# Left-over tokens loaded token by token, b_sg and g_ln loaded at another place, and a new order of the prologue

## The chip, the cores and the metric

The kernel runs on one core of a Trainium2 chip. Its engines work side by side, each through its own queue of instructions: TensorE (PE, with its weight loads PEld), VectorE (DVE), ScalarE (ACT), GpSimd (POOL) and SyncE (SP), which here issues nearly all DMAs. The metric is the device time of one execution in microseconds; the time of the kernel before is the median of three runs, 584.28 us (583.62 to 584.38).

## The reference

Eight heads of attention over pooled keys and values, followed by a gated MLP whose gate mixes the tokens. Cut to what is computed:

```python
# q, k, v: (8, 8, 576, 64)
k_p = k.reshape(B, H, 72, 8, D).mean(axis=3)      # 576 tokens pooled by 8: 72
v_p = v.reshape(B, H, 72, 8, D).mean(axis=3)
attn = softmax(q @ k_p.T / sqrt(D))               # over 72 pooled tokens
x = (attn @ v_p) -> (8, 576, 512)                 # heads side by side
h = gelu_tanh(x @ w_in)                           # w_in: (512, 1024)
u, v = h[..., :512], h[..., 512:]
v_n = (v - mean) / sqrt(var + 1e-6) * g_ln        # over the 512 of v
v_s = einsum('ts,bsd->btd', w_sg, v_n) + b_sg     # w_sg: (576, 576)
out = x + (u * v_s) @ w_out                       # w_out: (512, 512)
```

`w_in` and `w_out` arrive as 64-bit floats (their halves and quarters are loads of 1 MB), everything else as 32-bit.

## The kernel before, in words

**Tiling.** A batch is the unit of work. Four groups g of two heads each go through attention; 576 tokens are five tiles of at most 128. The 72 pooled tokens of a head don't fit two to a tile of 128, so each head's 72 are split into 64 main tokens and 8 left-overs. Main tokens of two heads fill 128 partitions. The left-overs of all eight heads of a batch are collected in one tile, `left`: k's on partitions 96 to 127 (two columns of 32 rows, one for each head of a pair), v's on partitions 64 to 95 (two columns, one for each half of the heads). `load_left` (L256) fills it with four DMAs of 64 KB, each of 32 rows of 2 KB. A row holds the eight tokens of one pooled one. The source is ordered head by head and, within a head, pooled token by pooled token; the partitions of the tile come in the same order.

**Products in three terms.** Matrices are split into a high part that PE multiplies fast and a low remainder, and a product is made of high times high, high times low and low times high. So there are many casts (ACT), subtractions (DVE, POOL) and conversions of the 64-bit weights (L196 to L207, on ACT, DVE, POOL, ACT, POOL in turn).

**Steps.** All work is cut into generator functions, one for each kind of step, and every `yield` ends a piece: A loads two K tiles, B two V tiles, C one group's q, E the left-overs. K pools K (on PE for batch 0, else on DVE, L315), and its third form K2 pools the left-overs of k and v (DVE, L315), transposes them and scales them into `kbd` (ACT, L345, L346). P does the same for V (POOL multiplies the left-overs with a mask, L381; `vl` L393 and L395 follows). Q transposes q. S makes the scores, the softmax (maximum L429, exponentials L441 or L446, sum, reciprocal L458, product L459) and copies the left-overs' probabilities into `el` (POOL, L465). L transposes `el` (PE, L135) and casts it into `lt` (ACT L476, L479, L480; DVE L482). T transposes the other probabilities (L493, L499). V multiplies with V into `x32` (L524) and `xhl`. H makes the v half of h with its normalization (DVE L569 to L575), U the u half, W the mixing over tokens with its eviction (L616, which reads `g_ln` as `gcol` and `b_sg` as `bbc`), O the output product, Z the transposition and the store. Lower-case entries treat the weights: lv, lu, lo load halves of w_in (v, u) and of w_out, `ls0` loads w_sg (five DMAs) and, in the kernel before, behind them `b_sg`, spread over all partitions (288 KB), and `g_ln` (2 KB, element by element); v, u, o, s are their conversions.

**The order.** It is written out by hand in two lists. `PROLOGUE` runs once: it holds batch 0, most of batch 1, the loads and the first pieces of batches 2 and 3, and all weights. `PERIOD` is then run for each further batch. Each entry `K2+1` advances step K2 of batch (period + 1) by one piece, and the instructions of a piece are appended to their engines' queues. At the end the program ties every instruction to the one before it on its engine, so that each engine works strictly in the order of the lists. That holds for SP too: a load that waits for a free buffer holds all loads behind it.

The order of loads on SP in the prologue is, before, A1+0, A0+0, lv0, E0+0, C0+0 to C3+0, lv1, B1+0, B0+0, ls0 (with b_sg and g_ln), E0+1, A0+1, lu0, A1+1, C0+1, C1+1, B0+1, lo0, lu1, B1+1, C3+1, C2+1, C1+2, C0+2, lo1, A1+2, E0+2, A0+2 and so on.

**The mask.** `mask` on partitions 64 to 95 has four columns; column a is 1/8 on the rows of head a of the half, and 0 elsewhere. It is made on POOL by a memset and two selects before the large memsets of `kbd`, `vbh` and others.

Of the kernel before, what the change touches and what calls it, by code (L numbers as in the profile page):

```python
# [35 lines left out]
O1+0 Q2+2 V2+1 V3+1 S0+2 B1+2 A0+3 O0+0 P1+2 Q1+2 S0+2 V3+1 S1+2 O0+0 A1+3 O1+0 P2+2 o3 S1+2 S1+2 S2+2 O2+0 O1+0 S2+2
C3+2 V0+1 S2+2 Z0+0 O2+0 S1+2 o3 V3+1 Z0+0 H2+1 H2+1 Q3+2 C0+3 O2+0 Z1+0 S0+2 T0+2
# [13 lines left out]
def tile_pooled_attn_gmlp(ctx: ExitStack, tc: tile.TileContext, q, k, v, w_in, g_ln, w_sg, b_sg, w_out, out):  # L51
# [46 lines left out]
    def mm(o, lhsT, rhs, start, stop):  # L98
# [112 lines left out]
    def load_wsg():  # L211
        st["ws"] = []
        for i in range(NT):
# [6 lines left out]
            st["ws"].append(w[:n])  # L220
        load(bbc, b_sg.rearrange("(o t) -> o t", o=1).broadcast_to([P, S]))
# [95 lines left out]
    def step_K(b, i):  # L317
# [23 lines left out]
        left = ps[:, 1, 96:P].rearrange("p (g j) -> p g j", g=G)  # L341
# [74 lines left out]
    def step_S(b, g):  # L416
# [47 lines left out]
        for h in range(2):  # L464
            nc.gpsimd.tensor_copy(st["el", b][:, :, JL * (2 * g + h):JL * (2 * g + h + 1)],  # L465
                                  ef[:, :, LEFT[h]:LEFT[h] + JL])
# [277 lines left out]
```

## Time and profile before

| | |
|---|---|
| median of three runs | 584.28 us (583.62 to 584.38) |
| the profiled execution's own time | 584.24 us |
| its span, first to last instruction | 582.5 us |
| granted TensorE clock, mean | 0.991 |
| PE busy | 554.7 us (95%), 3793 matmuls |
| DVE, ACT, POOL busy | 405.6, 351.9, 222.7 us |
| DMA moved | 46.34 MB, mean 80 GB/s |
| chain that ended last | PE 79%, DVE 10%, ACT 4%, DMA 3%, SP 2% |

Times in the profile count from the start of the span. "Busy" of an engine is the union of its instructions' times; an instruction row has start, duration, engine, source line, operation, the tile written and the tiles read, and in brackets the idle time before it with what ended it. Most matmuls come from one helper (L99), so they are told apart by their tiles: `mps` and `aps` are the two rings of PSUM tiles. All loads have line L155, so they go by tile: `kvraw` and `early` are K, V and q of the start, `left` the left-overs, `raw` the 64-bit weights, `stage` w_sg, `bbc` and `gcol` b_sg and g_ln. The busy share is an average over stages with different limits; a stage table shows each.

### The profile page before, as it was taken

Reading aid. Unit: us, or ns where it says so; the run is one execution under the profiler, and the core shown is the slowest. Engines: PE = TensorE matmul, PEld = TensorE weight load, DVE = VectorE, ACT = ScalarE, POOL = GpSimd, SP = SyncE. Lnnn points to the kernel's source line nnn. Section 1 sums busy time; section 2 is a strip of 40 time slices with the busy share of each in tenths; the row PEclk is TensorE's granted clock in tenths of the full one; section 3 lists DMA queues with packets and bytes.
Section 4 is the critical chain, followed back from the end, with each engine's and each line's share of the span. In section 5 each row is a group of like instructions: output and inputs, shape, how many; then the busy total and the mean of one; then the engine's idle time right before and its main releaser. Section 6 shows DMA issues by size and latency. Waiting matters only on the chain.

```text
span 582.5 us, 10319 instructions
## 1 busy us (share of the span) xinstructions
PE 554.7 (95%) x3793; PEld 522.9 (90%) x3793; DVE 405.6 (70%) x555; ACT 351.9 (60%) x1000; POOL 222.7 (38%) x301
## 2 busy tenths in 40 slices
PE   3698988999999999999999999999999999999995
PEld 3576788998999989999999989999999989998995
DVE  0579998988668795778667785688667765344434
ACT  2888776788547775497456765497456775412310
POOL 4365565833326131522416231532417131433230
PEclk9899998999999999999999999999999999999998
DMA  8988460462431634233441724134350211021105
GB/s 199 240 223 236 72 169 27 100 132 47 90 73 37 117 58 97 58 68 51 94 79 37 119 56 96 33 73 72 82 90 1 43 20 21 1 42 22 20 1 82
DMA packets 161282, 46.34 MB, mean 80 GB/s; under 512 B 148752, under 2 KB 148752, under 8 KB 161232
## 3 DMA queue, kind: packets, MB, share of 16 engines
q1 hardware_dynamic: 156464, 45.10, 37.9%
q10 hardware_dynamic: 4768, 0.59, 0.7%
q8 instruction: 30, 0.49, 0.4%
q14 instruction: 20, 0.16, 0.1%
HBM read 36.23 MB, written 9.44 MB: 78 GB/s over the span
## 4 chain that ended last, share of the span: by engine, by line
PE 79%; DVE 10%; ACT 4%; DMA 3%; SPq 2%; issue 1%; ACTq 0%; POOL 0%; DVEq 0%
PE mps L99 65%; PE aps L99 11%; PE aps L135 3%; ACT e L446 2%; SPq L155 2%; DMA left<-in_v 1%; DMA qraw<-in_q 1%; DVE e L459 1%; DVE bst L569 1%; DVE nmax L429 1%; DVE vg L575 1%; DVE vp L315 1%; DMA out<-y 1%; DVE ssum L449 1%; DVE qT L412 1%
## 5 line engine op out<-in xcount | busy, mean ns | idle before, releaser
L99 PE MATMUL mps<-xhl,wih 128*128 128x288 f32 x512 | 89.9, 298 | 0.0
L627 POOL TENSOR_TENSOR glo<-u,ghi 128x576 fp32r<-128x576 f32 x32 | 45.4, 1431 | 108.7 <-ACT ghi L625 106.8
L99 PE MATMUL mps<-wih,xhl 128*128 128x512 f32 x256 | 85.6, 400 | 0.1
L99 PEld LDWEIGHTS mps<-xhl,wih 128*128 128x128 f32 x512 | 75.8, 189 | 1.4
L446 ACT ACTIVATE e<-aps,nmax 128x72 f32<-128x72 f32 x240 | 73.4, 352 | 2.7 <-DVE nmax L429 2.4
L616 DVE SCALAR_TENSOR_TENSOR mps<-mps,gcol,bbc 128x576 f32<-128x576 f32 x32 | 26.4, 826 | 51.8 <-PE mps L99 51.7
L99 PEld LDWEIGHTS mps<-wih,xhl 128*128 128x128 f32 x256 | 48.1, 188 | 10.7 <-DVE x L659 0.3
L446 ACT ACTIVATION_READ_ACCUMULATOR e<-aps,nmax 128x1 f32 x240 | 57.1, 238 | 0.0
L99 PE MATMUL mps<-wsh,vhh 128*128 128x288 f32 x256 | 56.4, 302 | 0.0
L99 PE MATMUL mps<-wsl,vhh 128*128 128x288 f32 x256 | 55.4, 298 | 0.0
L99 PE MATMUL mps<-wsh,vhl 128*128 128x288 f32 x256 | 55.2, 297 | 0.0
L99 PE MATMUL mps<-xhl,wil 128*128 128x288 f32 x256 | 55.0, 296 | 0.0
L572 POOL TENSOR_TENSOR rstd<-mv,eps 128x1 f32<-128x1 f32 (+1 forms) x40 | 11.1, 277 | 114.0 <-DVE mv L570 104.5
L527 POOL TENSOR_TENSOR xhl<-x,xhl 128x576 fp32r<-128x576 f32 x32 | 45.3, 1430 | 23.9 <-ACT xhl L525 23.9
L575 DVE TENSOR_SCALAR vg<-vg,mv,rstd 128x512 f32<-128x512 f32 (+1 forms) x40 | 40.1, 1005 | 19.3 <-POOL rstd L573 19.3
L99 PE MATMUL mps<-ghi,woh 128*128 128x288 f32 x240 | 52.7, 301 | 0.0
L99 PE MATMUL mps<-ghi,wol 128*128 128x288 f32 x240 | 51.4, 295 | 0.0
L99 PE MATMUL mps<-glo,woh 128*128 128x288 f32 x240 | 51.4, 295 | 0.0
L99 PE MATMUL mps<-wil,xhl 128*128 128x512 f32 x128 | 50.6, 395 | 0.0
L565 ACT ACTIVATE vg<-mps 128x512 f32<-128x512 f32 x32 | 19.2, 599 | 45.4 <-PE mps L99 45.2
L585 POOL TENSOR_TENSOR vhl<-vg,vhh 128x512 fp32r<-128x512 f32 x32 | 42.2, 1319 | 9.4 <-ACT vhh L583 8.7
L625 ACT CAST ghi<-u 128x576 fp32r<-128x576 f32 x32 | 21.4, 673 | 39.5 <-DVE u L618 38.8
(158 smaller groups left out, 1423.9 us busy)
## 6 DMA issues: line engine op xcount, KB each, us to landing
out<-y SPq DMA_DIRECT2D x118, 72.0 KB
kvraw<-in_k SPq DMA_DIRECT2D x32, 256.0 KB
qraw<-in_q SPq DMA_DIRECT2D x112, 72.0 KB
kvraw<-in_v SPq DMA_DIRECT2D x28, 256.0 KB
raw<-in_moe_w_in SPq DMA_DIRECT2D x4, 1024.0 KB
raw<-in_moe_w_out SPq DMA_DIRECT2D x2, 1024.0 KB
stage<-in_moe_w_sg SPq DMA_DIRECT2D x4, 288.0 KB
left<-in_k SPq DMA_DIRECT2D x16, 64.0 KB
```

Of the source, the lines that this page charges most:

```text
L99: nc.tensor.matmul(o, lhsT, rhs, start=start, stop=stop)
L135: nc.tensor.transpose(ps[:rows, i * P:(i + 1) * P], src(i), ident if i < NT - 1 else swap)
L155: queue.dma_start(o, i)
L446: nc.scalar.activation(e[:, i, h], slots[i][:, h], AF.Exp, bias=nmax[:, i, h:h + 1], **acc)
L527: (nc.vector if b in LO_DVE else nc.gpsimd).tensor_tensor(xhl[:, 1, g], x32[:, g], xhl[:, 0, g].bitcast(F32), op=ALU.subtract)
L565: nc.scalar.activation(vg, o, AF.Gelu_apprx_tanh)
L572: nc.gpsimd.tensor_tensor(rstd, mv[:, 1:2], eps[:n, 1:2], op=ALU.add)
L575: nc.vector.tensor_scalar(vg, vg, mv[:, 0:1], rstd, op0=ALU.subtract, op1=ALU.mult)
L585: (nc.gpsimd if i < NT - 1 else nc.vector).tensor_tensor(lo, vg, hi.bitcast(F32), op=ALU.subtract)
L616: nc.vector.scalar_tensor_tensor(vs, vs, gcol[:, d:d + 1], bbc.rearrange("p (a n) -> p a n", a=2), op0=ALU.mult, op1=ALU.add)
L625: nc.scalar.copy(ghi[:, d], uf)
L627: nc.gpsimd.tensor_tensor(glo[:, d], uf, ghi[:, d].bitcast(F32), op=ALU.subtract)
```

## The change: what it does

- `load_left` reads its sources with the pooled token as the slowest dimension (8) and the head as the next (4), where it was head (4) and then token (8). The rows of `left` are ordered token by token, the size and the number of the DMAs stay.
- What follows from that order: the mask's columns pick every fourth row (made on DVE from the identity matrix by a sum over a strided view and a product, in place of the memset and two selects on POOL); K2's evacuation reads the transposed left-overs with a stride (L346); S copies the left-overs' probabilities to every fourth column of `el` (L465).
- `b_sg` and `g_ln` are loaded by a new function, called by a new entry `lb0` in the prologue.
- `PROLOGUE` is another order of the same steps with `lb0` added (352 entries for 351). `PERIOD` is untouched.

The order of loads on SP is after the change: A1+0, A0+0, lv0, E0+0, C0+0 to C3+0, B1+0, lv1, B0+0, ls0, A0+1, A1+1, lu0, E0+1, C0+1, C1+1, lo0, B0+1, lu1, C2+1, C3+1, B1+1, C1+2, C0+2, lo1, lb0, E0+2, A1+2, A0+2 and so on.

In VectorE's queue the first pooling of batch 1 (K0+1) now stands ahead of the subtraction of the first part of w_sg, both K poolings ahead of that of the left-overs (K2+1). At the end of batch 1's attention the last H tile's normalization and subtraction (H4+0) stand directly ahead of the two left-over subtractions (L0+1, L482), which follow each other, and the second w_out conversion (o0) stands ahead of them.

```diff
--- before.py
+++ after.py
@@ -21,20 +21,20 @@
 
 
 PROLOGUE = """
-A1+0 A0+0 lv0 v1 E0+0 v1 K0+0 C0+0 v0 K0+0 K2+0 C1+0 K1+0 C2+0 Q0+0 K1+0 K2+0 Q1+0 v0 Q0+0 K2+0 C3+0 S0+0 v1 v0 lv1
-Q2+0 v1 S0+0 B1+0 B0+0 Q3+0 Q1+0 v1 ls0 S1+0 v0 S1+0 Q2+0 S0+0 E0+1 S1+0 S0+0 S2+0 Q3+0 A0+1 v3 T0+0 S1+0 S2+0 S3+0
-S0+0 v3 S3+0 S3+0 S2+0 P0+0 lu0 v0 S2+0 S3+0 v2 v3 S3+0 A1+1 P1+0 S1+0 S2+0 S3+0 P2+0 T0+0 s3 v3 T1+0 S3+0 S3+0 L0+0
-s3 v3 v2 C0+1 v2 s4 s3 T1+0 K0+1 L0+0 s4 C1+1 V0+0 B0+1 v2 K2+1 lo0 T2+0 s4 s1 V0+0 s1 T2+0 u1 v2 V1+0 V1+0 V2+0 T3+0
-s2 u1 V2+0 K1+1 V0+0 T3+0 K2+1 u0 lu1 K2+1 s2 s1 u1 V3+0 Q0+1 V3+0 u0 Q1+1 s2 V1+0 S0+1 S0+1 S0+1 S1+1 u1 V2+0 V1+0
-V3+0 u0 S1+1 V2+0 S0+1 S1+1 u0 V0+0 H0+0 H2+0 u1 S1+1 S0+1 S0+1 H0+0 P0+1 S0+1 H2+0 S1+1 u3 s0 s0 V3+0 T0+1 H0+0 U1+0
-H2+0 s0 U1+0 S1+1 H1+0 T0+1 u0 B1+1 H0+0 P1+1 C3+1 u3 P2+1 C2+1 H2+0 H0+0 S1+1 S0+1 Q2+1 u2 u2 H2+0 H0+0 Q3+1 H1+0
-P2+1 T0+1 H4+0 P2+1 H4+0 u2 H4+0 S2+1 H3+0 H2+0 S3+1 S2+1 H4+0 S1+1 C1+2 S2+1 u2 u2 u3 C0+2 H1+0 H3+0 S2+1 U0+0 u3
-S3+1 u3 S3+1 S2+1 H4+0 S3+1 H3+0 U0+0 P2+1 o0 H1+0 U2+0 H4+0 S3+1 S2+1 S3+1 S2+1 U3+0 S2+1 lo1 H1+0 S3+1 o1 A1+2 o1
-U2+0 E0+2 H4+0 S3+1 H1+0 L0+1 H3+0 T1+1 H3+0 L0+1 H4+0 L0+1 H3+0 Q0+2 o1 U3+0 W2+0 L0+1 o1 V0+1 o1 o3 o0 T1+1 K1+2
-W2+0 T1+1 o3 W3+0 T2+1 o0 o0 W3+0 o0 V0+1 o2 V1+1 o2 T2+1 o2 T2+1 W0+0 A0+2 V1+1 V2+1 o3 K0+2 o2 W2+0 V1+1 T3+1 B0+2
-W1+0 K2+2 V2+1 W2+0 T3+1 W0+0 W0+0 T3+1 W3+0 o2 K2+2 K2+2 V3+1 C2+2 W0+0 W1+0 W3+0 P0+2 W1+0 W1+0 S0+2 O0+0 S0+2 V1+1
-O1+0 Q2+2 V2+1 V3+1 S0+2 B1+2 A0+3 O0+0 P1+2 Q1+2 S0+2 V3+1 S1+2 O0+0 A1+3 O1+0 P2+2 o3 S1+2 S1+2 S2+2 O2+0 O1+0 S2+2
-C3+2 V0+1 S2+2 Z0+0 O2+0 S1+2 o3 V3+1 Z0+0 H2+1 H2+1 Q3+2 C0+3 O2+0 Z1+0 S0+2 T0+2
+A1+0 A0+0 lv0 E0+0 v1 C0+0 v1 K0+0 K1+0 C1+0 K2+0 Q0+0 C2+0 v0 K1+0 C3+0 K0+0 K2+0 Q0+0 v1 K2+0 v0 Q1+0 S0+0 B1+0 v0
+Q1+0 Q2+0 v1 Q3+0 v0 Q2+0 S0+0 S0+0 lv1 S1+0 S1+0 S0+0 S1+0 v1 Q3+0 S1+0 B0+0 S2+0 S2+0 ls0 v0 v3 S0+0 T0+0 v3 S2+0
+S3+0 P0+0 S3+0 A0+1 S1+0 A1+1 S3+0 S3+0 lu0 S2+0 E0+1 v3 S2+0 S3+0 P1+0 S3+0 s3 T0+0 S3+0 v2 C0+1 T1+0 P2+0 v3 S3+0
+v2 s3 L0+0 s4 T1+0 K0+1 v2 C1+1 lo0 L0+0 v2 s3 V0+0 s4 s1 v3 T2+0 K1+1 V0+0 v2 T2+0 V1+0 s4 u1 V1+0 T3+0 K2+1 V2+0 u0
+s2 T3+0 V2+0 u1 V1+0 K2+1 V3+0 K2+1 s1 B0+1 Q0+1 s2 Q1+1 V0+0 u0 V3+0 s1 V2+0 u0 S0+1 s2 S1+1 S0+1 V3+0 u0 S0+1 S0+1
+u1 S1+1 u1 S1+1 H0+0 u0 H2+0 S1+1 H0+0 lu1 S0+1 S0+1 u1 P0+1 H2+0 S0+1 S1+1 u3 s0 T0+1 s0 H0+0 H1+0 H2+0 S1+1 s0 C2+1
+Q2+1 C3+1 H0+0 V1+0 S0+1 H0+0 u3 Q3+1 B1+1 V0+0 H2+0 U1+0 P1+1 H1+0 S1+1 u2 u3 H2+0 U1+0 u2 H3+0 V3+0 T0+1 T0+1 H0+0
+P2+1 C1+2 P2+1 S1+1 S2+1 V2+0 H4+0 u2 H2+0 S2+1 S2+1 H3+0 u2 u3 S3+1 H4+0 u2 C0+2 H1+0 P2+1 S2+1 lo1 U2+0 u3 H4+0
+S3+1 H3+0 S3+1 S3+1 U2+0 o1 U0+0 H4+0 P2+1 o0 S2+1 U3+0 S2+1 S3+1 S2+1 H1+0 lb0 S3+1 E0+2 S2+1 S3+1 A1+2 H1+0 H3+0
+H3+0 S3+1 H4+0 L0+1 o1 o0 A0+2 H1+0 H4+0 U0+0 H4+0 L0+1 H4+0 T1+1 H3+0 L0+1 o1 W2+0 L0+1 o0 U3+0 W2+0 o1 V0+1 W3+0 o0
+T1+1 K0+2 T1+1 V0+1 T2+1 K1+2 o0 o1 V1+1 o3 W0+0 T2+1 o3 o2 B0+2 T2+1 o3 W3+0 T3+1 o3 o2 B1+2 K2+2 V1+1 V2+1 W0+0
+T3+1 o2 W1+0 Q1+2 T3+1 V2+1 Q0+2 K2+2 V1+1 C2+2 W2+0 W0+0 W0+0 W1+0 W3+0 o2 C3+2 V3+1 K2+2 S0+2 W2+0 W1+0 S0+2 W1+0
+O1+0 W3+0 O1+0 o2 P1+2 V3+1 S1+2 o3 O0+0 Q2+2 S0+2 C0+3 A1+3 S1+2 O1+0 S0+2 O0+0 O0+0 O2+0 Z1+0 V0+1 S2+2 V1+1 P0+2
+O2+0 S2+2 V2+1 Q3+2 S1+2 P2+2 O2+0 V3+1 V3+1 S2+2 S1+2 Z0+0 H2+1 H2+1 S0+2 T0+2 A0+3 Z0+0
 """.split()
 PERIOD = """
 H1+0 H1+0 P2+1 U3+0 T0+1 Z1-1 H2+0 H2+0 H2+0 H1+0 C1+2 S2+1 H1+0 P2+1 S3+1 O3-1 H2+0 V2+0 S3+1 O3-1 H1+0 Z2-1 K1+2
@@ -109,12 +109,9 @@
     tiny = const.tile([P, NT, 2], F32, name="tiny")
     nc.gpsimd.memset(tiny, 1e-9)
     mask = const.tile([96, 4], F32, name="mask")
-    nc.gpsimd.memset(mask, 1.0 / POOL)
     sl = mask[64:96, :]
-    nc.gpsimd.affine_select(out=sl, in_=sl, compare_op=ALU.is_ge, fill=0.0, base=0,
-                            pattern=[[-JL, 4]], channel_multiplier=1)
-    nc.gpsimd.affine_select(out=sl, in_=sl, compare_op=ALU.is_ge, fill=0.0, base=JL - 1,
-                            pattern=[[JL, 4]], channel_multiplier=-1)
+    nc.vector.tensor_reduce(out=sl, in_=ident[64:96, 64:96].rearrange("p (j a) -> p a j", a=4), axis=AX.X, op=ALU.add)
+    nc.vector.tensor_scalar(sl, sl, 1.0 / POOL, None, op0=ALU.mult)
     kbd = const.tile([P, G, 2 * SP], F32, name="kbd")
     nc.gpsimd.memset(kbd, 0.0)
     vbh = const.tile([P, G, P], F32R, name="vbh")
@@ -218,6 +215,8 @@
                 w = per.tile([P, S], F32, name="stage", tag="tmp")
             load(w[:n], w_sg[i * P:i * P + n, :])
             st["ws"].append(w[:n])
+
+    def load_vectors():
         load(bbc, b_sg.rearrange("(o t) -> o t", o=1).broadcast_to([P, S]))
         load(gcol, g_ln.rearrange("(c p) -> p c", p=P))
 
@@ -256,12 +255,12 @@
     def load_left(b):
 
         t = per.tile([P, 2, POOL * D], F32, name="left")
-        src = k[b].rearrange("(g h) (j r) d -> h g j (r d)", h=2, r=POOL)
+        src = k[b].rearrange("(g h) (j r) d -> h j g (r d)", h=2, r=POOL)
         for h in range(2):
-            load(t[96:P, h], src[h, :, JM:SP])
-        src = v[b].rearrange("h (j r) d -> h j (r d)", r=POOL)
+            load(t[96:P, h], src[h, JM:SP])
+        src = v[b].rearrange("h (j r) d -> j h (r d)", r=POOL)
         for gp in range(2):
-            load(t[64:96, gp], src[4 * gp:4 * gp + 4, JM:SP])
+            load(t[64:96, gp], src[JM:SP, 4 * gp:4 * gp + 4])
         st["left", b] = t
 
     def load_q(b, g):
@@ -338,7 +337,7 @@
         nc.tensor.transpose(ps[:, 1, 0:P], lp.rearrange("p h d -> p (h d)"), ident)
         yield
         main = ps[:, 0, 0:2 * P].rearrange("p (g j) -> p g j", g=G)
-        left = ps[:, 1, 96:P].rearrange("p (g j) -> p g j", g=G)
+        left = ps[:, 1, 96:P].rearrange("p (j g) -> p g j", g=G)
         c = D ** -0.5 / POOL
         for h in range(2):
             r = slice(D * h, D * h + D)
@@ -462,7 +461,7 @@
         if ("el", b) not in st:
             st["el", b] = per.tile([P, NT, H * JL], F32, name="el")
         for h in range(2):
-            nc.gpsimd.tensor_copy(st["el", b][:, :, JL * (2 * g + h):JL * (2 * g + h + 1)],
+            nc.gpsimd.tensor_copy(st["el", b].rearrange("p t (n j a) -> p t n j a", n=2, a=4)[:, :, g // 2, :, 2 * (g % 2) + h],
                                   ef[:, :, LEFT[h]:LEFT[h] + JL])
 
     def step_L(b, _):
@@ -693,6 +692,8 @@
             i = int(name[2])
             if name[1] == "s":
                 load_wsg()
+            elif name[1] == "b":
+                load_vectors()
             else:
                 load_w(name[1], i)
         else:
```

## The prediction

> **What bounds the kernel now.** I read the page first, then the busy time by stage, then the chain of waits, then the instruction rows of the stages in which the TensorE isn't the limit. The page gives the span; the stage table (columns: stretch, its length, busy us and instructions of PE, PEld, DVE, ACT, POOL, then granted clock, DMA share, GB/s) tells which stretch has room.
>
> ```profile
> span 582.5 us, 10319 instructions
> ```
> ```profile
> 0.00:12.60 12.60, 4.42 (x22) 4.46 (x23) 0.00 (x0) 1.96 (x3) 5.93 (x24) 1.00 0.84 209
> 12.60:40.20 27.60, 20.88 (x150) 18.27 (x149) 17.20 (x28) 24.68 (x91) 11.96 (x17) 0.94 0.91 228
> 40.20:52.50 12.30, 10.84 (x57) 8.05 (x56) 12.15 (x12) 10.69 (x22) 6.88 (x6) 1.00 0.87 184
> 52.50:93.50 41.00, 36.43 (x229) 32.09 (x228) 38.58 (x57) 29.42 (x50) 25.55 (x36) 1.00 0.55 141
> 93.50:137.35 43.85, 43.49 (x296) 41.46 (x297) 38.76 (x50) 32.64 (x102) 24.28 (x23) 0.96 0.46 90
> 226.10:292.10 66.00, 65.97 (x461) 62.98 (x461) 49.21 (x67) 43.09 (x133) 22.94 (x31) 1.00 0.38 73
> ```
>
> From 93.5 us on the PE has no room: 43.49 of 43.85 us, then 65.97 of 66.00 in a period. The order of the periods isn't edited, so what the change is worth is the shift of the instant, now 93.5, from which PE runs unbroken. Before it the limit moves. Until 12.6 VectorE has no data. From 12.6 to 40.2 DMA is 91% busy and VectorE idles 10.4 of 27.6 us. From 40.2 VectorE is the limit: 12.15 of 12.30, then 38.58 of 41.00 us, with PE idle 1.46 and 4.57 us beside it. The chain of waits says the same: early on a transfer of left-overs, and the last piece before PE's unbroken run begins as VectorE's subtraction of 92.61 (further below) ends.
>
> ```profile
> 6.40 7.88 DMA left<-in_v
> ...
> 93.50 1.68 PE aps L99 x8
> ```
>
> So an idle microsecond taken from VectorE in its first 93 us is worth up to a microsecond at the end. VectorE's rows show two idles that a transfer ended: 0.53 us before the left-overs' pooling of batch 0 and 2.67 us before the first K pooling of batch 1. After the second there is no gap.
>
> ```profile
> 13.08 0.69 DVE L200 SCALAR_TENSOR_TENSOR top<-raw,top 128x512 int32<-128x512 int32 x1
> 14.30 1.92 DVE L315 TENSOR_REDUCE lp<-left 64x128 f32<-64x1024 f32 x1 [0.53 <-DMA left<-in_v]
> ...
> 36.77 0.74 DVE L160 TENSOR_TENSOR wsl<-mps,wsh 128x576 fp32r<-128x576 f32 x1
> 40.19 1.98 DVE L315 TENSOR_REDUCE kp<-kvraw 128x128 f32<-128x1024 f32 x1 [2.67 <-DMA kvraw<-in_k]
> 42.19 1.92 DVE L315 TENSOR_REDUCE lp<-left 64x128 f32<-64x1024 f32 x1
> ...
> 52.52 0.89 DVE L429 TENSOR_REDUCE nmax<-aps 128x10 f32<-128x720 f32 x1
> ```
>
> Why the K transfer was late stands in SP's rows of issue, and in what the DMA engines did from 30 to 36 us (two strips of 40 slices of 0.15 us: busy tenths, GB/s):
>
> ```profile
> 27.33 0.33 SPq L155 DMA_DIRECT2D bbc<-in_moe_b_sg  x1
> 28.59 0.38 SPq L155 DMA_DIRECT2D gcol<-in_moe_g_ln  x1
> 29.77 1.42 SPq L155 DMA_DIRECT2D left<-in_k  x2
> 31.56 1.50 SPq L155 DMA_DIRECT2D left<-in_v  x2
> 33.19 1.32 SPq L155 DMA_DIRECT2D kvraw<-in_k  x2
> 34.56 0.59 SPq L155 DMA_DIRECT2D raw<-in_moe_w_in  x1
> ```
> ```profile
> DMA  9999999989899953523345323333123463699999
> GB/s 369 261 215 231 246 184 184 200 170 247 231 217 140 244 89 75 102 106 119 120 87 128 140 84 140 110 110 109 55 109 123 164 191 109 232 423 382 341 246 219
> ```
>
> For 5.86 us (33.19 less 27.33) SP issues b_sg, g_ln and four left-over loads ahead of batch 1's K. From 32 to 35 us only about 0.3 of the engines work, at some 110 GB/s: a left-over load runs on four or five of 16, and the rest wait for SP.
>
> **The change, part by part.**
>
> *Left-overs on eight engines.* The same 256 KB a batch, from a source whose slowest dimension is 8 tokens and no longer 4 heads (k) or 4 heads of a half (v). For batch 0, VectorE is free at 13.77 (13.08 + 0.69) and waits until 14.30. Half the bytes on each busy engine must win 0.53 of the 7.88 us that the chain gives the last of these loads. Bounds: 0 and −0.53; what stands before it on VectorE doesn't change, so no more. I take −0.53, as the four loads trail one another on the same engines. The Trainium skill, "DMA: Bandwidth & Descriptors", section "Why a DMA increments its semaphore by 16 and not by 1", has the sync queue use the largest number up to 16 that divides the slowest dimension on both sides. That makes 4 before and 8 now, and the 0.3 busy share agrees for the 4; by it the sum is the same, and the slower rival below loses its second condition.
>
> *b_sg and g_ln late, left-overs of batch 1 behind K and w_in.* SP now goes from w_sg straight to the four K loads, so the first is issued about 5.9 us sooner. At the 7.00 us from issue to use that is seen (33.19 to 40.19) the data are there by 34.3. VectorE would want them at 36.3: the K pooling now stands ahead of the subtraction at 36.77, and the 0.53 of above is off. The wait goes whole: −2.67 (bounds 0, if another transfer takes its place, and −2.67). What is late next is the transfer behind: the first u half of w_in, then the left-overs. w_in was issued at 34.56 and ScalarE got it at 44.12:
>
> ```profile
> 44.12 0.69 ACT L196 ACTIVATE top<-raw 128x512 f32<-128x512 f32 x1 [1.45 <-DMA raw<-in_moe_w_in]
> ```
>
> With four loads of 0.65 us ahead it is now issued near 30.0, and by the same 9.56 us lands at 39.6. The left-overs follow at 30.6 to 33.2 and by the 7.88 us of the chain land at 41.1. VectorE comes to them at 41.8 (36.3, two K poolings of 1.98, two subtractions of 0.74): hidden, by 0.7 us only. b_sg and g_ln are first read at the first W eviction (97.6 us, L616); their new place on SP is behind the second w_out load and ahead of batch 2's left-overs, whose buffer VectorE frees at 82.1 (the last reader, below). That leaves over 10 us: 0, and if it is gone the eviction waits on VectorE with all that follows.
>
> *PE has to follow.* A gain of 3.2 us on VectorE needs as much room on PE: it idles 1.46 + 4.57 us between 40.2 and 93.5. Its waits there are for VectorE, for ScalarE (which stood 1.45 us for w_in) and for POOL, so they shrink with their causes. Price 0.
>
> *The order of the rest of the prologue.* The list holds the same steps plus one, the vector load. Up to the first softmax of batch 1, VectorE has the same set of steps; from there to the left-overs' last subtraction of batch 1 it gains one more w_out conversion (0.42 + 0.69) and loses a transposition (0.78): +0.33. The last stretch in front of PE's 93.5:
>
> ```profile
> 81.45 0.68 DVE L395 TENSOR_TENSOR vl<-left,vl 32x512 fp32r<-32x512 f32 x1
> ...
> 86.05 0.42 DVE L199 TENSOR_SCALAR top<-top 128x512 int32<-128x512 int32 x1
> 86.50 0.74 DVE L200 SCALAR_TENSOR_TENSOR top<-raw,top 128x512 int32<-128x512 int32 x1
> ...
> 90.52 0.75 DVE L482 TENSOR_TENSOR lt<-aps,lt 32x576 fp32r<-32x576 f32 x1 [1.14 <-ACT lt L480]
> 91.30 0.78 DVE L412 STREAM_TRANSPOSE qT<-qraw 128x576 f32<-128x576 f32 x1
> 92.61 0.75 DVE L482 TENSOR_TENSOR lt<-aps,lt 32x576 fp32r<-32x576 f32 x1 [0.53 <-ACT lt L480]
> ```
>
> The first wait of 1.14 can go, since more VectorE work now stands between the last softmax and it; the second of 0.53 grows by the transposition that filled it, 0.78. Together 0.33 − 1.14 + 0.78, about 0. Bounds: −1.7 (both waits go) and +2.5 (a rival, below).
>
> *Mask, strided copies, later periods.* Memset and two selects of the mask leave POOL, which idles 6.96 us before its first instruction on data (first row below); two small VectorE operations come, about 0.2 us each by the nearest small row (the 226 ns copy below), into the 12.6 us before VectorE's first data: 0, and without that cover 0.5. The copy of left-over probabilities now writes every fourth element; bounds 0 and, were its 226 ns doubled, 0.23 a copy, two copies a step. In a period POOL has 43 of 66 us free; 0. The periods' left-over loads lie under a DMA share of 0.38: 0.
>
> ```profile
> 13.92 1.28 POOL L202 TENSOR_TENSOR top<-top,raw 128x512 int32<-128x512 int32 x1 [6.96 <-DVE top L200]
> ```
> ```profile
> L465 POOL COPY el<-e 128x40 f32<-128x40 f32 x64 | 12.4, 226 | 52.3 <-ACT vg L565 27.7 <-DVE e L459 24.5
> ```
>
> **Sum.** −0.53 − 2.67 = −3.20 us. The profiled execution took 584.24 us (span 582.5, 1.74 around it), 0.04 under the median of 584.28: 584.24 − 3.20 = 581.04, so **581.0**.
>
> **Rivals.** *A half-clock stretch goes too (faster).* The stage table shows a stretch near half speed just where PE becomes the limit:
>
> ```profile
> 85.00:93.50 8.50, 5.43 (x41) 4.97 (x40) 6.67 (x11) 4.59 (x9) 5.11 (x7) 1.00 0.27 83
> 94.00:98.00 4.00, 4.00 (x21) 4.00 (x20) 3.97 (x3) 2.70 (x5) 2.64 (x3) 0.57 0.02 4
> ```
>
> It follows 8.50 us in which PE idled 3.07, and costs 4.00 × 0.43 = 1.72 us of PE. Should the new order close the idle ahead of it, the time is 581.0 − 1.7 = 579.3. For it: PE's 3.07 us hang on the left-overs' softmax, copies and subtractions, which come sooner relative to its own work; against: VectorE sets the pace there, so that PE idles in any case. The Trainium skill, "TensorE: Matmul & The Clock Gate", section "Part 1: The HAM clock gate", has the clock halve after an idle window of some 3.4 us and stay so for about as long; the length agrees (4.00 us at 0.57 are 3.4 us at half), but PE's idle ahead of it was shorter than that.
>
> *Given back at the end of batch 1 (no change).* Batch 1's last stretch puts the last H tile's normalization, cast (0.62 us on ScalarE) and subtraction, and then both left-over subtractions back to back, directly ahead of PE's unbroken run. If VectorE stands for ScalarE in each (0.62, and 2 × 1.28 for two pairs of 0.63-us copies less the 0.53 seen), that is up to 2.6: 581.0 + 2.6 = 583.6. For it: VectorE and ScalarE alternate there already (1.14 and 0.53). Against: PE's four W matmul groups run in that time.
>
> *The left-overs become the late transfer (slower).* Place: VectorE's left-over pooling of batch 1, now behind 1 MB of w_in. If the engines' pace and not SP's issue set w_in's landing, it stays at 44.1, as 0.5 MB of K goes ahead of it for the 0.55 MB that leave. If moreover eight engines give nothing over four, the left-overs need the 2.8 us of the trough and land at 46.9. VectorE stands there, and all behind it. From that pooling to the softmax's first step it has about 8.0 us (pooling 1.92, two conversions of 1.11 to 1.97, two transpositions of 0.78, two subtractions of 0.74): 54.9 for 52.5, which is +2.4 and 586.6. It decides from a landing after 44.5 (52.5 less 8.0). For it: DMA is 0.91 busy until 40. Against: the trough at 32 to 35, in which engines had nothing to do.
>
> **How the numbers follow.** A measurement of this kernel tells 0.2%, 1.2 us: 583.1 to 585.4 is no change. Chances: 0.55 for 581.0 (with 579.8 to 582.6), 0.15 for 579.3 and below, 0.15 for 583.6, 0.15 for the slower case, of which a fifth stays within 0.2%. Faster 0.70, same 0.18, slower 0.12. The range is 578.0 to 584.9: its lower end holds the closed clock stretch with 1.3 us of PE's 3.07 us of idle, its upper end all of the no-change case and little of the slower one.
>
> **What would show it.** Right: VectorE's K pooling of batch 1 with no wait for a transfer and near 36 us; its left-over pooling with none either; the first softmax of batch 1 near 49.3; PE's unbroken run from about 90.3; periods of 66.0 us. The first step is wrong if the left-over pooling of batch 0 still begins after 14.2; the second, if a wait of over 2 us for a transfer stands before any pooling; the third, if PE's last long idle ends at 93 or later with VectorE early. A period that isn't 66.0 us makes all of it wrong.

## The result, and the profile after

The changed kernel takes **587.77 us** in the median of 15 runs (584.84 to 589.41), the kernel before 584.27 beside it (15 runs, 581.97 to 585.32): a ratio of 1.0067, 95% interval 1.0055 to 1.0080. It is slower by 3.5 us; the forecast was 3.2 us faster.

The profiled execution of the changed kernel took 584.84 us, the fastest of its 15 runs. Its trace therefore shows the loss smaller than it is at the median; a second trace of the same kernel stands among the experiments. Lines after the removed mask code are one to three lower than before (the pooling L315 is now L314, the conversion L199 and L200 now L196 and L197, the left-over subtraction L482 now L481).

The busy time by stage, columns as in the table of before:

```profile
span 583.1 us, 10319 instructions
```
```profile
0.00:12.60 12.60, 4.17 (x20) 4.20 (x21) 2.39 (x4) 2.86 (x4) 5.37 (x21) 1.00 0.87 218
12.60:40.20 27.60, 20.74 (x157) 17.82 (x156) 20.14 (x29) 24.77 (x92) 13.07 (x18) 1.00 1.04 245
40.20:52.50 12.30, 12.12 (x66) 9.90 (x66) 11.52 (x14) 10.91 (x21) 8.84 (x6) 1.00 0.93 247
52.50:93.50 41.00, 34.66 (x213) 30.08 (x211) 38.49 (x52) 27.21 (x46) 24.43 (x36) 0.97 0.48 108
93.50:137.35 43.85, 42.40 (x289) 40.34 (x290) 36.97 (x50) 33.09 (x103) 22.78 (x22) 0.95 0.42 84
226.10:292.10 66.00, 65.97 (x461) 63.01 (x460) 49.20 (x68) 43.11 (x133) 23.02 (x31) 1.00 0.38 73
```

Up to 52.5 us VectorE and PE got further than before: VectorE was busy 20.14 us for 17.20 in the second stage, and PE 12.12 for 10.84 in the third. In the fourth, PE did 34.66 us of work for 36.43, and in the fifth 42.40 for 43.49. A period is untouched (65.97 of 66.00). So the loss lies between 52.5 us and the end of the prologue.

VectorE's rows at the front:

```profile
13.08 1.97 DVE L314 TENSOR_REDUCE lp<-left 64x128 f32<-64x1024 f32 x1 [0.20 <-DMA left<-in_v]
...
35.65 1.96 DVE L314 TENSOR_REDUCE kp<-kvraw 128x128 f32<-128x1024 f32 x1
...
40.96 1.98 DVE L314 TENSOR_REDUCE lp<-left 64x128 f32<-64x1024 f32 x1 [0.16 <-DMA left<-in_v]
...
49.47 0.91 DVE L428 TENSOR_REDUCE nmax<-aps 128x10 f32<-128x720 f32 x1
```

In this trace the front did what was forecast: the K pooling of batch 1 at 35.65 without a wait, the first softmax maximum of batch 1 at 49.47, 3.05 us ahead of the 52.52 of before.

VectorE's rows in the last stretch of the prologue, and GpSimd's beside them:

```profile
84.14 4.53 DVE L196 TENSOR_SCALAR top<-top 128x512 int32<-128x512 int32 x1
88.70 0.69 DVE L197 SCALAR_TENSOR_TENSOR top<-raw,top 128x512 int32<-128x512 int32 x1
89.31 0.53 DVE L574 TENSOR_SCALAR vg<-vg,mv,rstd 64x512 f32<-64x512 f32 x1
90.53 1.01 DVE L584 TENSOR_TENSOR vht<-vg,vht 64x512 fp32r<-64x512 f32 x1 [0.69 <-ACT vht L582]
91.70 0.75 DVE L481 TENSOR_TENSOR lt<-aps,lt 32x576 fp32r<-32x576 f32 x1 [0.16 <-ACT lt L479]
93.78 0.75 DVE L481 TENSOR_TENSOR lt<-aps,lt 32x576 fp32r<-32x576 f32 x1 [1.34 <-ACT lt L479]
```
```profile
83.62 1.00 POOL L572 TENSOR_TENSOR rstd<-rstd,mhalf 64x1 f32<-64x1 f32 x1
84.61 2.52 POOL L584 TENSOR_TENSOR vhl<-vg,vhh 128x512 fp32r<-128x512 f32 x2
87.09 1.29 POOL L199 TENSOR_TENSOR top<-top,raw 128x512 int32<-128x512 int32 x1
```

The first row is a conversion of w_out. The eleven other rows of this form in the trace take 0.39 to 0.43 us (0.42 in the row that the prediction quotes). Here it lasts 4.53. VectorE waits for no semaphore in that time; the row counts as busy. GpSimd works without a pause from 83.62 to 88.38 (87.09 + 1.29), and the conversion ends 0.29 us later. Behind it in VectorE's queue are the last H tile's normalization (89.31) and subtraction (90.53), for which PE waits:

```profile
91.59 0.85 PE L99 MATMUL mps<-wth,vht 128*128 128x288 f32 x2 [3.52 <-DVE vht L584]
...
94.68 0.58 PE L99 MATMUL aps<-ah,vbh 128*128 128x288 f32 x1 [1.75 <-DVE lt L481]
```
```profile
90.70:97.70 7.00, 4.35 (x17) 4.04 (x18) 5.44 (x6) 5.07 (x9) 2.46 (x3) 0.51 0.01 2
```

The row at 94.68 is the one that stood at 93.50 before: 3.05 us gained in front of 49.47, and 4.23 given back between it and here (45.21 us for 40.98). In the kernel before, the longest waits of PE here were 1.39 us, and 1.69 us ahead of the row at 93.50 (from its rows, and from its waits: total, times, longest):

```profile
86.76 0.63 PE L135 MATMUL aps<-ident,el 128*64 128x128 f32 x4 [1.39 <-POOL el L465]
```
```profile
PE aps L99 <- DVE lt L482: 1.7, 1, 1.7
```

The granted clock drops to half at 90.86, inside the first of the two waits, and stays there for 6.83 us; before, the half-clock stretch at this place lasted 3.41 us, from 94.21.

### The profile page after: what moved, and what is told of

Same layout as the page of the kernel before. It is cut to its first block, busy times and chain, and to the rows that moved or that the text cites. A ratio compares the mean times of both kernels' runs of the same rounds, so it can differ in the third digit from the quotient of the medians.

```text
span 583.1 us, 10319 instructions
## 1 busy us (share of the span) xinstructions
PE 553.3 (95%) x3793; PEld 521.5 (89%) x3793; DVE 408.9 (70%) x557; ACT 351.8 (60%) x1000; POOL 223.4 (38%) x298
## 3 DMA queue, kind: packets, MB, share of 16 engines
q1 hardware_dynamic: 156592, 45.10, 38.1%
## 4 chain that ended last, share of the span: by engine, by line
PE 79%; DVE 8%; DMA 6%; ACT 3%; SPq 1%; issue 1%; ACTq 0%; POOL 0%; DVEq 0%
PE mps L99 65%; PE aps L99 11%; PE aps L132 3%; DMA left<-in_k 3%; DMA stage<-in_moe_w_sg 2%; SPq L152 1%; DMA early<-in_v 1%; DVE top L196 1%; DVE e L458 1%; DVE nmax L428 1%; DVE bst L568 1%; DVE vp L314 1%; DMA out<-y 1%; DVE ssum L448 1%; DVE vg L574 1%
## 5 line engine op out<-in xcount | busy, mean ns | idle before, releaser
L99 PE MATMUL mps<-ghi,wol 128*128 128x288 f32 x240 | 51.3, 295 | 0.0
```

Of the source, the lines that this page charges most:

```text
L99: nc.tensor.matmul(o, lhsT, rhs, start=start, stop=stop)
```

## The experiments

The theory: the order of the late prologue makes VectorE stand behind GpSimd, and that costs more than the loads win. Rivals: the loads themselves cost, or the early part of the new order does. All kernels were timed against the kernel before on the same chip. "Softmax" is the start of batch 1's first softmax maximum, "stretch" the time from there to the start of batch 1's first weighted sum of v on PE (the row at 93.50 before, at 94.68 after), "to next" the time from softmax to the same instruction of batch 2. Times in us, from one trace each; ratio from the timed runs.

| kernel | median | ratio (95%) | softmax | stretch | to next |
|---|---|---|---|---|---|
| before | 584.27 | 1 | 52.52 | 40.98 | 105.47 |
| after | 587.77 | 1.0067 (1.0055-1.0080) | 49.47 | 45.21 | 109.37 |
| e1 after, again | 587.82 | 1.0065 (1.0043-1.0087) | 53.88 | 45.14 | 110.47 |
| e2 after, o0 later | 587.21 | 1.0053 (1.0039-1.0067) | 52.58 | 43.94 | 108.75 |
| e3 after, old layout | 589.41 | 1.0091 (1.0073-1.0108) | 52.36 | 45.10 | 110.48 |
| e4 before, new layout | 583.53 | 0.9988 (0.9974-1.0002) | 51.61 | 41.98 | 106.48 |
| e5 after, less GpSimd work | 584.70 | 1.0009 (0.9995-1.0023) | 50.52 | 42.24 | 106.56 |
| e6 before, GpSimd thrice | 584.04 | 0.9991 (0.9977-1.0005) | 51.35 | 43.60 | 106.62 |
| e7 before, both loads new | 581.83 | 0.9959 (0.9942-0.9976) | 50.42 | 40.97 | 105.48 |
| e8 the same, again | 581.92 | 0.9969 (0.9957-0.9981) | 50.00 | 40.99 | 105.49 |
| e9 new order, then old | 582.92 | 0.9983 (0.9969-0.9998) | 50.22 | 41.03 | 105.53 |
| e10 before, three places | 583.81 | 0.9989 (0.9972-1.0006) | 51.83 | 41.63 | 105.32 |
| e12 e7, one pooling later | 582.09 | 0.9972 (0.9956-0.9989) | 53.59 | 40.97 | 104.60 |
| e13 e10, power op ahead | one run, 583.30 | - | 51.23 | 42.19 | 105.68 |
| e14 after, no power op | 587.32 | 1.0057 (1.0026-1.0089) | 50.99 | 44.79 | 110.24 |

**e1: the changed kernel once more, unedited.**

> The changed kernel, unedited, for a second trace and a second ratio on another day's chip. Theory (a conversion on VectorE stands behind GpSimd late in the prologue): its row for the second w_out conversion at about 84 us again lasts over 2 us instead of 0.4, PE's unbroken run begins after 93.5, ratio 1.005 to 1.009. Rival (the loss varies from run to run for a reason that the first trace didn't catch): the conversion lasts under 1 us, or the loss shows in another row, ratio still about 1.007.

Measured: 1.0065, with a trace at the slow end (590.48 us). VectorE's rows:

```profile
39.08 1.93 DVE L314 TENSOR_REDUCE kp<-kvraw 128x128 f32<-128x1024 f32 x1 [2.83 <-DMA kvraw<-in_k]
...
45.56 1.96 DVE L314 TENSOR_REDUCE lp<-left 64x128 f32<-64x1024 f32 x1 [1.38 <-DMA left<-in_v]
...
53.88 0.90 DVE L428 TENSOR_REDUCE nmax<-aps 128x10 f32<-128x720 f32 x1
...
88.48 4.52 DVE L196 TENSOR_SCALAR top<-top 128x512 int32<-128x512 int32 x1
```

Two different things show. The front isn't fixed: the K pooling waited 2.83 us here, as long as in the trace of before, and the softmax began at 53.88, later than before. The 4.52-us conversion and the stretch of 45.14 are the same to 0.1 us. The late loss came back in the second trace, the front gain of 3.05 us did not.

**e2: the second w_out conversion (o0) moved behind the left-over subtractions.**

```diff
-H3+0 S3+1 H4+0 L0+1 o1 o0 A0+2 ... H3+0 L0+1 o1 W2+0 L0+1 o0 U3+0 W2+0 o1 V0+1 W3+0 o0
+H3+0 S3+1 H4+0 L0+1 o1 A0+2 ... H3+0 L0+1 o1 W2+0 L0+1 U3+0 W2+0 o0 o1 V0+1 W3+0 o0 o0
```

> The changed kernel with one piece moved: the second w_out conversion's VectorE pair goes back behind both left-over subtractions of batch 1 and the first W eviction, as it stood before the change. Theory: the 4.53 us stand goes, PE's waits of 3.5 and 1.75 us before 95 shrink to under 3 in sum, the half-clock stretch of 6.8 us shortens to 3.4 or nothing; ratio to the kernel before 0.993 to 0.998. Rival (another step of the change costs the time): ratio stays 1.005 to 1.008.

Measured: 1.0053, stretch 43.94: the ratio is the rival's, and PE's two waits sum to 4.62 us (2.02 and 2.60). With the conversion gone from that place, the next VectorE instruction stood in its stead, behind the same two subtractions and the same sum of GpSimd:

```profile
87.70 3.99 DVE L574 TENSOR_SCALAR vg<-vg,mv,rstd 64x512 f32<-64x512 f32 x1 [0.44 <-POOL rstd L572]
```

This normalization lasts 0.53 in the trace of after. So it is not the conversion as such: whichever instruction of this kind comes up beside that run of GpSimd stands.

**e3 and e4: the layout of the left-overs alone.** e3 is the changed kernel with the old layout, e4 the kernel before with the new one.

```diff
-        src = k[b].rearrange("(g h) (j r) d -> h j g (r d)", h=2, r=POOL)
+        src = k[b].rearrange("(g h) (j r) d -> h g j (r d)", h=2, r=POOL)
...
```

> The changed kernel with the left-overs laid out as before (loads on four engines, mask on GpSimd, no strided copies); the new order and the late b_sg and g_ln stay. Theory: the layout isn't what costs; VectorE's left-over poolings of batch 0 and 1 begin 0.3 to 1.5 us later, the late stand stays; ratio 1.006 to 1.011. Rival (strided copies or poolings of the new layout cost): faster than the changed kernel, ratio under 1.004.

> The kernel before with the new layout of the left-overs alone (eight engines, mask from the identity, strided copies); order and b_sg, g_ln as before. Theory: the trough from 32 to 35 us shortens little, as SP's issue of the four loads fills it, the left-over pooling of batch 0 starts 0.3 to 0.5 us earlier and K of batch 1 up to 1 us earlier; ratio 0.997 to 1.000. Rival (the layout costs): ratio 1.003 or more.

Measured: 1.0091 and 0.9988. In e3 the left-over pooling of batch 1, second behind w_in in the new order, waited longer than in any trace with the new layout (0 to 1.70):

```profile
44.18 1.99 DVE L317 TENSOR_REDUCE lp<-left 64x128 f32<-64x1024 f32 x1 [3.18 <-DMA left<-in_v]
```

The layout isn't the loss: without it the new order is no faster, and 1.6 us slower at the median than e1 (587.82).

**e5: the changed kernel with 2.5 us less GpSimd work in that run.**

```diff
+        if b == 0 and i in (1, 3):
+            nc.scalar.copy(lo, vg)
+            yield
+            return
         (nc.gpsimd if i < NT - 1 else nc.vector).tensor_tensor(lo, vg, hi.bitcast(F32), op=ALU.subtract)
```

> The kernel after, with batch 0's low part of v written for two of its four token tiles by a plain ScalarE copy instead of GpSimd's subtraction (so those two low remainders are left out of the computation). GpSimd loses two 1.26 us instructions of the run behind which VectorE's second conversion of the output weights stood for 4.53 us. Theory (VectorE stands for the whole of GpSimd's gapless run): that conversion lasts 1.8 to 2.2 us, the stretch from the softmax maximum of batch 1 to the start of its v projection is 42.5 to 43.2 us in place of 45.2, ratio to before 1.001 to 1.004. Rival (the conversion is slow for another reason, such as its own operand): still about 4.5 us, stretch 45, ratio 1.0065.

Measured: 1.0009, stretch 42.24. The stand is gone, more fully than expected:

```profile
85.18 0.42 DVE L196 TENSOR_SCALAR top<-top 128x512 int32<-128x512 int32 x1
85.63 1.84 DVE L197 SCALAR_TENSOR_TENSOR top<-raw,top 128x512 int32<-128x512 int32 x1
```

The conversion takes 0.42, the instruction after it 1.84 beside GpSimd's sum. It did not stand for the rest of GpSimd's run either, a power operation and that sum without a pause. Of the 4.23 us by which the stretch had grown, 2.97 (45.21 less 42.24) went with the two subtractions. The other 1.26 us are mainly the extra conversion (0.42 and the 1.84) and longer waits for ScalarE (0.69, 0.13 and 1.33 us where the kernel before has 1.14 and 0.53), less a transposition of 0.78 and some shorter rows. That GpSimd's two subtractions cause the stand is shown; that its length alone does so was the next question.

**e6, e10, e13: the kernel before with a longer run of GpSimd.** e6 repeats the subtraction for token tile 1, e10 writes it to two more places (chunks of the low output weights, overwritten later), e13 puts a power operation ahead of e10's run.

```diff
+        for _ in range(3 if (b, i) == (0, 1) else 1):                     # e6
 (nc.gpsimd if i < NT - 1 else nc.vector).tensor_tensor(lo, vg, hi.bitcast(F32), op=ALU.subtract)
+        if (b, i) == (0, 1):                                              # e10
+            for junk in (wol[:, 2], wol[:, 3]):
+                nc.gpsimd.tensor_tensor(junk, vg, hi.bitcast(F32), op=ALU.subtract)
```

> The kernel before, with the GpSimd subtraction that writes the low part of v for token tile 1 of batch 0 issued three times with the same result: 2.5 us more of GpSimd's gapless run and nothing else. Theory: VectorE's normalization near 87, which stood 1.50 us in the kernel before, stands about 4 us, the v projection of batch 1 starts 2 to 2.6 us later, ratio 1.003 to 1.006. Rival (GpSimd's work is hidden and does not hold VectorE): the row stays at or under 1.6 us and the ratio is 1.000.

> The kernel before with two more GpSimd subtractions behind the one for token tile 1 of batch 0, each written to a place of its own that is overwritten later, so that no GpSimd instruction of the three waits for the one ahead of it (in the run with the same place written three times, 78 ns lay between them). Theory (a run of GpSimd instructions without a gap keeps VectorE out to its end): VectorE's normalization near 87 stands about 4 us in place of 1.50. Rival (VectorE gets its turn after one GpSimd instruction, with or without the 78 ns): it stays at 1.5 us.

> The kernel before with the three GpSimd subtractions in a row of the earlier run, and one more 128x1 power operation of GpSimd ahead of them. Theory (behind a power operation a run of GpSimd keeps VectorE out to its end): VectorE's normalization near 87 stands 4 us or more. Rival (the power operation has nothing to do with it): 1.5 us as in the run without it.

Measured: in all three the theory's number for VectorE's stand failed. GpSimd's and VectorE's rows of e10:

```profile
85.97 1.72 POOL L585 TENSOR_TENSOR vhl<-vg,vhh 128x512 fp32r<-128x512 f32 x1
87.65 3.16 POOL L588 TENSOR_TENSOR wol<-vg,vhh 128x512 fp32r<-128x512 f32 x2
```
```profile
86.47 1.50 DVE L575 TENSOR_SCALAR vg<-vg,mv,rstd 128x512 f32<-128x512 f32 x1
88.00 1.66 DVE L585 TENSOR_TENSOR vht<-vg,vht 64x512 fp32r<-64x512 f32 x1
```

GpSimd runs from 85.97 to 90.81 without a gap, longer than in the changed kernel, and VectorE's normalization stands 1.50 us as it did in the kernel before, for one GpSimd instruction. The next VectorE instruction stands for one more. Here the two engines take turns. e6 shows the same (1.51, then 1.65). In e13 the normalization took 0.54: it was over (86.41) before the power operation was (86.45), so it did not meet the run of subtractions. The next VectorE instruction did, and stood for one GpSimd instruction:

```profile
86.44 1.72 DVE L588 TENSOR_TENSOR vht<-vg,vht 64x512 fp32r<-64x512 f32 x1
```

None of the three is slower than before (0.9991, 0.9989, and one run of 583.30). In e6 the weighted sum of batch 1 did begin 2.62 us later after its softmax, as the theory said, but not through the normalization: VectorE waited 2.31 us for ScalarE's cast of w_sg at 63.47, and PE 2.17 us at 92.44 for GpSimd's longer work. That of batch 2 began only 1.15 us later: the delay was mostly absorbed.

**e14: the changed kernel without the power operation.** What the two standing cases (after, e2) share and e10 lacks is a power operation at the head of GpSimd's run.

```diff
-        nc.gpsimd.tensor_tensor(rstd, rstd, mhalf[:n], op=ALU.pow)
+        nc.gpsimd.tensor_tensor(rstd, rstd, mhalf[:n], op=ALU.mult if (b, i) == (0, NT - 1) else ALU.pow)
```

> The kernel after with the power operation in the normalization of batch 0's last 64 tokens replaced by a multiplication of the same form, so that these tokens are scaled wrongly; all else as it was. Theory (power operation): VectorE's second conversion of the output weights at 84 stands at most 1.7 us in place of 4.53, the stretch from the softmax maximum of batch 1 to its v projection is 42 to 43 us, ratio to before 1.000 to 1.003. Rival (the order of the subtractions does it, whatever is ahead): 3.8 to 4.6 us, stretch 44.5 to 45.2, ratio 1.005 to 1.008.

Measured: 1.0057, stretch 44.79.

```profile
85.62 4.15 DVE L196 TENSOR_SCALAR top<-top 128x512 int32<-128x512 int32 x1
```

The stand is still there. The power operation isn't its cause.

**e7, e8, e9: the loads without the late order.** e7 (and e8, once more on another chip) is the kernel before in its old order with the new layout and the two vectors loaded late. e9 is the changed kernel up to batch 0's first gating step, 137 entries of the order, then the old order.

```diff
-S3+1 u3 S3+1 ... U3+0 S2+1 lo1 H1+0 S3+1 o1 A1+2 o1
+S3+1 u3 S3+1 ... U3+0 S2+1 lo1 H1+0 S3+1 lb0 o1 A1+2 o1
```

> The kernel before in its own order, with the two other parts of the change: the token-by-token layout of the left-over tokens and the two vectors loaded late, behind the third softmax step of batch 1. Theory (loads are a gain, the new order is the loss): K pooling of batch 1 starts up to 2.4 us earlier, the late stretch stays at 41 to 42 us, ratio 0.995 to 0.999. Rival (the loads gain nothing that lasts): ratio 0.999 to 1.001.

> The kernel before in its own order with the two loading changes once more, on whichever chip it falls. Theory (the loading part of the change is a gain that repeats): ratio 0.994 to 0.998, late stretch 41 to 42 us. Rival (the first run's 0.996 was the landing of one execution): ratio 0.999 to 1.001.

> The kernel after up to the first step of batch 0's gating, and from there the order of the kernel before. Theory (the loss lies wholly in the order of the late prologue): stretch from the softmax maximum of batch 1 to its v projection 41 to 42 us, gain ahead of it 0 to 3 us, ratio 0.993 to 0.999. Rival (the new order of the early prologue costs by itself): ratio 1.000 or more with the late stretch at 41 to 42.

Measured: 0.9959, 0.9969 and 0.9983. The first row is e7's K pooling of batch 1, the second its stretch by engine (columns as in the stage table), the third and fourth the same stretch of e9 and of after:

```profile
36.89 1.95 DVE L314 TENSOR_REDUCE kp<-kvraw 128x128 f32<-128x1024 f32 x1
```
```profile
50.42:91.39 40.97, 36.36 (x229) 32.05 (x228) 38.54 (x57) 29.65 (x50) 25.79 (x36) 1.00 0.54 131
```
```profile
50.22:91.25 41.03, 36.75 (x231) 32.20 (x229) 38.60 (x57) 29.78 (x51) 26.28 (x37) 1.00 0.52 121
```
```profile
49.47:94.68 45.21, 37.69 (x231) 32.80 (x229) 42.32 (x58) 30.13 (x51) 27.46 (x38) 0.96 0.50 120
```

With the old order behind it, the loading part is a gain of 2.2 to 2.4 us at the median, and the stretch is 41.0 us again. The changed kernel has one more instruction on VectorE in that stretch than e7 and 3.78 us more busy time; the stand alone, 4.53 us for 0.42, is more than that. e7 beats both kernels: the loads were the good half of the change, the late order the bad one.

The stand is not the whole cost of the new order. e5, without it, is still 2.9 us slower than e7 at the median (584.70 for 581.83), of which the traces show 1.27 in the stretch (42.24 for 40.97); the rest isn't located. e9 is 1.1 us slower than e7 (582.92), with intervals that just overlap, so a small cost of the early part of the new order isn't excluded.

**e12: e7 with one K pooling of batch 2 moved.** PE waited 1.48 us at 97.92 in e7 for a subtraction that stood behind a 2.07-us pooling.

```diff
-... o3 o0 T1+1 K1+2
-W2+0 T1+1 o3 W3+0 ...
+... o3 o0 T1+1
+W2+0 T1+1 K1+2 o3 W3+0 ...
```

> The kernel before in its own order with the two loading changes, and the second K pooling of batch 2 (VectorE, 2.07 us at 93.47) moved behind the step that makes the low part of the second head group's transposed weights of batch 1. Theory (TensorE waited 1.48 us at 97.92 for that low part because VectorE was pooling): the wait goes, the rest starts 1 to 1.5 us earlier, ratio to before 0.992 to 0.996, below that of the same kernel without the move in this call. Rival (the pooling then holds what comes next): ratio equal to that of the same kernel without the move.

Measured: 0.9972, not to be told from e8's 0.9969. In the trace the wait is gone and "to next" is 104.60 for 105.49, 0.9 us shorter; but this execution's front was late (softmax at 53.59). A gain of 0.9 us is in the trace and can't be told at the median.

## Why the prediction was wrong

*Left-overs on eight engines (-0.53).* Right in kind. The wait at batch 0's pooling was 0.20 in the profiled run, not zero. The layout's whole worth is 0.12% in the old order (e4, interval from -0.26 to +0.02) and 0.26% in the new (e3 less e1).

*b_sg and g_ln late (-2.67).* The mechanism was right, the size too large. In the trace of after the wait is gone and 35.65 and 49.47 fall within 0.7 and 0.2 us of the forecast. But the 2.67 was one execution's. The same wait in two other kernels whose front is that of before (e6, e10), from one trace each:

```profile
38.76 1.97 DVE L315 TENSOR_REDUCE kp<-kvraw 128x128 f32<-128x1024 f32 x1 [0.81 <-DMA kvraw<-in_k]
```
```profile
38.90 1.95 DVE L315 TENSOR_REDUCE kp<-kvraw 128x128 f32<-128x1024 f32 x1 [0.48 <-DMA kvraw<-in_k]
```

In e13 it is absent. So the term's mean is near 1 us by these four traces (2.67, 0.81, 0.48, 0), and in the changed kernel the wait can come back (2.83 in e1, 1.16 in e2). Both load terms together, measured where nothing else changes (e7, e8), are 2.2 to 2.4 us where 3.20 was forecast.

*The order of the rest of the prologue (about 0, bounds -1.7 and +2.5).* This is the step that failed: the term was put at about 0 and measured +4.23 us. Its count of instructions was right: the first left-over wait went (1.14 to 0.16), the second grew (0.53 to 1.34, where 0.78 was added in the sum). What it left out is that a VectorE instruction's duration depends on what GpSimd does beside it. The growth lies beyond the upper bound, and 2.97 us of it go when two GpSimd subtractions go (e5). The sign was in the profile of before, in a row that the prediction didn't weigh: a normalization that takes 0.53 to 0.57 us at its four other places in that stretch and lasted almost three times as long beside GpSimd's subtraction.

```profile
87.17 1.50 DVE L575 TENSOR_SCALAR vg<-vg,mv,rstd 128x512 f32<-128x512 f32 x1
```
```profile
86.67 1.72 POOL L585 TENSOR_TENSOR vhl<-vg,vhh 128x512 fp32r<-128x512 f32 x1
```

The Trainium skill, "SBUF — State Buffer", section "Who interferes with whom", says why such rows exist: VectorE in certain forms and GpSimd share one port pair, the one that issues first has it for the whole instruction, and the other is fully blocked. The 1.50 here and in e10, which end with one GpSimd instruction, agree. It doesn't say what happens when GpSimd's next instruction is ready at once; the 4.53 against the 1.50 of e10 shows that both outcomes occur.

*PE has to follow (0).* Wrong with the step above: PE's waits didn't shrink, they became 3.52 and 1.75 us, where before had 1.39 and 1.69, and its half-clock stretch went from 3.41 us to 6.83 in after and e2, to 10.24 in e1, e3 and e14. How much of the loss is the clock shows in "to next" less "stretch", the time from one batch's weighted sum to the next one's. In after, e2, e1, e3 and e14 it is 64.16, 64.81, 65.33, 65.38 and 65.45 us, with 3.01, 4.39, 5.65, 5.83 and 5.88 us of half clock in it: about 0.45 us more for each of them. Before has 64.49 with 3.41. So behind the weighted sum the clock costs up to 1.0 us, and in the trace of after nothing. In the stretch ahead of it, where the 4.23 us lie, PE waits for VectorE.

*The rival "a half-clock stretch goes too".* In e7 it did go, and nothing came of it. The 4.00 us behind the start of the weighted sum in e7:

```profile
91.89:95.89 4.00, 4.00 (x33) 4.00 (x32) 3.97 (x3) 2.68 (x5) 2.64 (x3) 1.00 0.02 4
```

At full clock PE does 33 matmuls there, where the kernel before did 21 at 0.57. Yet "to next" is 105.48 for 105.47: PE then waits for VectorE's subtraction (the wait that e12 moves).

```profile
97.92 0.66 PE L132 MATMUL aps<-ident,e 128*128 128x128 f32 x4 [1.48 <-DVE al L498]
```

Four traces with the old late order and full clock (e4, e7, e8, e9) have this wait, 1.47 to 1.49 us, and before, at half clock, has none, so its half clock took the place of the wait. (In e6, also at full clock, the weighted sum starts later and the wait is 0.35.) The rival's 1.7 us weren't to be had; PE wasn't yet the limit at 93.5.

*The two other rivals.* "Given back at the end of batch 1" named the right place, the last H tile's normalization, cast and subtraction ahead of PE's run, but for the most part the wrong engine. ScalarE stood 5.83 us for VectorE's normalization, while VectorE's own waits for ScalarE came to 2.19 us (0.69, 0.16 and 1.34) where before had 1.67; the rival was priced at 2.6 us.

```profile
89.88 0.62 ACT L582 CAST vht<-vg 64x512 fp32r<-64x512 f32 x1 [5.83 <-DVE vg L574]
```

"The left-overs become the late transfer" happened in part: with the old layout the wait is 3.18 (e3), with the new one 0 to 1.70.

*The strided copies and the mask (0).* The copy of left-over probabilities went from 226 to 266 ns, the lower half of its bounds; e4, which has it in the old order, isn't slower. Right.

```profile
L464 POOL COPY el<-e 128x40 f32<-128x40 f32 x64 | 13.7, 266 | 54.7 <-ACT vg L564 27.5 <-DVE e L458 27.2
```

*What the median says.* The profiled run of before lay at its median, the profiled run of after 2.9 us under its own. Over all traces of the new order the front is worth little: with the new layout the softmax starts at 49.47, 53.88, 52.58, 50.52, 50.22 and 50.99 (mean 51.3), in the four kernels with the front of before at 52.52, 51.35, 51.83 and 51.23 (mean 51.7), one trace each. Some 0.4 less there and 3.9 to 5.0 more to the next batch (after, e1, e3) make 3.5 to 4.6; 3.5 was measured.

**What stays open.** Why VectorE stood for three to four GpSimd instructions in a row in the changed kernel (and e1, e2, e3, e14), and for one in e6, e10, e13 and the kernel before. The length of GpSimd's run isn't enough (e10), gaps of 78 ns in it change nothing (e6 beside e10), and a power operation isn't needed (e14). The VectorE instructions differ too (128 rows in e10, 64 in e2, another operation in after), and that was not varied alone; no run told apart what decides. Open as well is where the rest of e5's 2.9 us over e7 goes.

## What to carry to other kernels

Before moving instructions between queues, list the rows of VectorE that last longer than their like, and look at what GpSimd does in that time: such a duration belongs to the pair, not to the instruction, and a new order can multiply it. A wait for a transfer read from one trace is one draw; traces of kernels that leave that part alone show how far it scatters. When a change bundles a data layout, a load's place and a searched order, time the parts apart: here the loads won 0.3 to 0.4%, and the order lost 1% against them.

## What the runs showed of the hardware

A VectorE conversion of 0.39 us lasted 4.15 to 4.53 while GpSimd worked without a pause beside it, in every trace that has this order (after, e1, e3, e14), and the profile books the time as VectorE busy. With a longer GpSimd run elsewhere the engines took turns instruction by instruction (1.50, 1.66).

The half-clock stretches of PE in the prologue come in lengths of 3.41, 6.83 and 10.24 us in these traces, one, two and three times 3.41. PE need not idle that long for one: in the 3.41 us ahead of the drop at 94.21 in the kernel before it was busy half of the time (its wait is 1.69 us).

The first K pooling of batch 1 needs two loads. They were issued at 25.43 and 26.32 in after and used at 35.65 without a wait; in e1 they were issued at 26.36 and 28.22 and used at 39.08, after 2.83 us of waiting: 1.9 us of later issue became at least 3.4 us of later arrival.
